# One transpose a head for both key tiles in the last eight attention blocks

## The chip, the cores and the metric

The kernel runs on one core of a Trainium2 chip. The metric is the device time of one execution in microseconds. Three runs of the kernel before gave 677.7, 679.01 and 679.52 us; the median is 679.01 us. The engines are named as in the profile: PE (TensorE, matrix products), PEld (its weight loads), DVE (VectorE), ACT (ScalarE), POOL (GpSimd), SP (the queue that issues the DMAs).

## The reference

Windowed attention with sinks, followed by two feed-forward layers over 1536 tokens of width 512:

```python
keep = (pos[None, :] < n_sink) | ((rel >= 0) & (rel < window))   # rel = query - key, n_sink 4, window 128
scores = np.where(keep, scale * (q @ k.T), -1e9)                 # 2 batches, 8 heads, 768 positions, head size 64
a = softmax(scores)                                              # with 1e-9 added to the sum
x = (a @ v) as [1536, 512]
h = x @ w_in;  x = (h * clip(h + 3, 0, 6) / 6) @ w_out           # first layer, 512 -> 2048 -> 512
h = x @ w_in2; out = (max(h, 0) + log1p(exp(-abs(h)))) @ w_out2  # second layer
```

A query at position q with window 128 sees keys q-127 to q. For a tile of 128 queries these lie in two key tiles of 128: its own (keys at or below the query's place in the tile) and the one before (keys above that place). Every place from 0 to 127 is used in exactly one of the two.

## The kernel before, in words

Attention works in 24 blocks (two heads by 256 queries), each of two units of 128 queries, so 48 units, numbered n from 0 to 47. A unit makes, for each of its two heads, a score tile of 288 columns: 128 keys of the tile before, 32 sink places, 128 keys of its own tile.

- `e_S` (line 410): four matmuls write the scores `s` to PSUM; `at_exp` (line 350) takes them off on DVE with the mask added and the row's extreme (line 355), and ACT takes the exponent with a running sum (line 359).
- `at_N` (line 364): the sum is inverted; the sink part `Ps` and the probabilities `Pt` are scaled (lines 376 to 385), from unit 16 on one head on DVE and one on ACT, in some units both on ACT.
- `e_T` (line 425): per head two PE transposes, one a key tile, into one PSUM bank `tv` (in the trace `etv`); after the second head ACT copies the whole bank to `EPT` (line 443). Units at the start of a sequence have only one key tile, and one transpose a head.
- `e_Ts` (line 447): two transposes of the sink parts and their copy. `e_V` (line 455): twelve or fewer products with v, four with the sinks' v, and the result to `X` in two parts (ACT and DVE).

`tv`, the sinks' transposes and the output of `e_V` share a pool that has a single bank (`NTV` is 1) once the first layer runs, so each has to be emptied before the next is written.

The first turns (scores of units 0 to 18) run alone at the start. The other units are woven into the first layer (`m1_h`, `m1_y`): every matmul of the layer advances a counter (`tick`), and the parts of a unit are emitted at fixed counts (`turn`, with the offsets `TH` and `TS`). The products of PE are pinned to the order in which they are written; DVE, ACT and POOL get theirs from a scheduler that orders by its own estimate of when inputs are ready. Meanwhile the weights arrive as 64-bit numbers, and each tile is turned into floats by three DVE steps (lines 28, 29, 32), two ACT steps and one POOL subtraction. The masks are made at the very start by `build_masks` (line 276) on DVE. After the attention ends, the second layer follows (`m2_h`, `m2_e`, `m2_g`, `m2_o`).

Of the kernel before, what the change touches and what calls it, by code (L numbers as in the profile page):

```python
# [8 lines left out]
F32 = mybir.dt.float32  # L9
# [3 lines left out]
AF = mybir.ActivationFunctionType  # L13
ALU = mybir.AluOpType
# [4 lines left out]
SK = 32  # L19
# [158 lines left out]
def window_attention_hardswish_softplus(  # L178
# [17 lines left out]
    nc = tc.nc  # L196
# [3 lines left out]
    P = 128  # L200
    NP = H // 2
# [6 lines left out]
    scale = 1.0 / float(D) ** 0.5  # L208
# [32 lines left out]
    negm = const.tile([P, 2 * NPU], F32, name="negm")  # L241
# [14 lines left out]
    def acopy(out_, in_, scale_=1.0, bias=0.0):  # L256
        nc.scalar.activation(out=out_, in_=in_, func=AF.Copy, scale=scale_, bias=bias)  # L257


    def pin(ins):  # L260
        return tc.keep_in_program_order(ins)
# [14 lines left out]
    def build_masks(raw, pos, mt):  # L276
        rel, col = pos[:, 0:2 * P], pos[:, 2 * P:3 * P]
        tmp = mt.tile([P, 3, 2 * P], F32, name="mtmp")
        vf = const.tile([P, 2, 2], F32, name="vf")
        nc.vector.tensor_copy(vf, raw)  # L280
        neg = const.tile([P, 2, 2], F32, name="vneg")
        nc.vector.tensor_scalar(neg, vf, 0.0, 4294967296.0, op0=ALU.is_lt, op1=ALU.mult)
        nc.vector.tensor_tensor(out=val, in0=vf[:, :, 0], in1=neg[:, :, 0], op=ALU.add)
        nc.vector.scalar_tensor_tensor(
            out=val, in0=vf[:, :, 1], scalar=4294967296.0, in1=val, op0=ALU.mult, op1=ALU.add
        )
        ns, w = val[:, 0:1], val[:, 1:2]
        k2, kn, kk = tmp[:, 0, :], tmp[:, 1, :], tmp[:, 2, :]
        big = -NEG

        def put(dst, src):
            nc.vector.tensor_scalar(dst, src, big, -big, op0=ALU.mult, op1=ALU.add)
        nc.vector.tensor_scalar(k2, rel, w, None, op0=ALU.is_lt)
        nc.vector.scalar_tensor_tensor(out=k2, in0=rel, scalar=0.0, in1=k2, op0=ALU.is_ge, op1=ALU.mult)
        nc.vector.tensor_scalar(kn[:, 0:P], col, ns, None, op0=ALU.is_ge)
        nc.vector.tensor_scalar(kn[:, P:P + SK], col[:, 0:SK], ns, None, op0=ALU.is_lt)
        m = masks[0]
        nc.vector.tensor_tensor(out=kk[:, P:], in0=k2[:, P:], in1=kn[:, 0:P], op=ALU.mult)
        put(m[:, 0:SK], kn[:, P:P + SK])
        put(m[:, SK:SK + P], kk[:, P:])  # L300
        nc.vector.memset(m[:, SK + P:], NEG)
        nc.vector.tensor_tensor(out=kk[:, 0:P], in0=k2[:, 0:P], in1=kn[:, 0:P], op=ALU.mult)
        for t, src in ((1, kk), (2, k2)):
            m = masks[t]
            put(m[:, 0:P], src[:, 0:P])
            put(m[:, P + SK:], k2[:, P:])
            put(m[:, P:P + SK], kn[:, P:P + SK])
        nc.vector.tensor_scalar(flagc[:, 0:1], ns, float(SK), None, op0=ALU.is_gt)
        nc.vector.tensor_scalar(flagc[:, 1:2], w, 1.0, None, op0=ALU.is_lt)
        nc.vector.tensor_scalar(flagc[:, 2:3], w, 128.0, None, op0=ALU.is_gt)  # L310


    AT = {}
# [21 lines left out]
    def blk(k):  # L335
        g, p = divmod(k, NP)
        b, i = divmod(g, BPB)
        return g, p, b, i

    def cols(n):  # L340
        k, i = divmod(n, 2)
        g, p, b, ib = blk(k)
        t = 2 * ib + i
        if t == 0:
            return t, 0, SK + P + SK
        if ib == 0:
            return t, SK, 2 * P + SK
        return t, i * (P + SK), 2 * P + SK

    def at_exp(n, h, s, Pt):  # L350
        t, c0, w = cols(n)
        u = 2 * n + h
        if h == 0:
            A["sum", n] = AT["ep"].tile([P, 2], F32, name="sm", tag="sm")
        nc.vector.tensor_tensor_reduce(  # L355
            out=Pt[:, h, :w], in0=s[:, :w], in1=masks[min(t, 2)][:, :w], scale=-scale, scalar=3.0e38,
            op0=ALU.add, op1=ALU.min, accum_out=negm[:, u:u + 1],
        )
        nc.scalar.activation(  # L359
            out=Pt[:, h, :w], in_=Pt[:, h, :w], func=AF.Exp, scale=-1.0, bias=negm[:, u:u + 1],  # L360
            accum_out=A["sum", n][:, h:h + 1],
        )

    def at_N(n):
        t, c0, w = cols(n)
        Pt = A["P", n]
        sm = A.pop(("sum", n))
        nc.vector.tensor_scalar(sm, sm, 1e-9, None, op0=ALU.add)
        i = nc.vector.reciprocal(sm, sm)
        if n < 4 * NP:  # L370
            stand(i)
        cs = 0 if t == 0 else P
        Ps = AT["ep"].tile([P, 2, SK], F32, name="Ps", tag="Ps")

        early = n < 4 * NP
        (nc.gpsimd if early else nc.vector).tensor_tensor(
            out=Ps, in0=Pt[:, :, cs:cs + SK], in1=sm[:, :, None].to_broadcast([P, 2, SK]), op=ALU.mult)
        A["Ps", n] = Ps
        for h in range(2):
            if early:  # L380
                nc.gpsimd.tensor_scalar(Pt[:, h, :w], Pt[:, h, :w], sm[:, h:h + 1], 1.0, op0=ALU.mult, op1=ALU.mult)
            elif h == 1 or (n < 8 * NP and n % 2 == 1):
                acopy(Pt[:, h, :w], Pt[:, h, :w], sm[:, h:h + 1])
            else:
                nc.vector.tensor_scalar(Pt[:, h, :w], Pt[:, h, :w], sm[:, h:h + 1], None, op0=ALU.mult)

# [21 lines left out]
    def e_S(n):  # L410
        k, i = divmod(n, 2)
        t, c0, w = cols(n)
        r = A["e", k]
        Pt = AT["ep"].tile([P, 2, 2 * P + SK], F32, name="Pt", tag="Pt")
        A["P", n] = Pt
        ss = [AT["eps_s"].tile([P, 512], F32, name="s", tag="s") for _ in range(2)]
        for h in range(2):
            x = r[h * D:(h + 1) * D]
            mm(out=ss[h][:, :w], lhsT=x[:, i * P:(i + 1) * P], rhs=x[:, UB + c0:UB + c0 + w], start=True, stop=True)
        for h in range(2):  # L420
            at_exp(n, h, ss[h], Pt)
        if i == 1:
            A.pop(("e", k))

    def e_T(n, h):
        k, i = divmod(n, 2)
        t, c0, w = cols(n)
        Pt = A["P", n]
        if h == 0:
            A["tv", n] = AT["eps_t"].tile([P, 2, 2, P], F32, name="etv", tag="tv")  # L430
            if i == 0:
                A["EPT", k] = (AT["ept"].tile([P, 2, 4, P], F32, name="EPT", tag="EPT"),
                               AT["ept"].tile([2 * SK, 2, P], F32, name="EPTs", tag="EPTs"))
        PT, _ = A["EPT", k]
        tv = A["tv", n]
        for j, c in ([(1, SK)] if t == 0 else [(0, 0), (1, P + SK)]):
            pin(nc.tensor.transpose(tv[:, h, j, :], Pt[:, h, c:c + P], ident))
        if h == 0:
            return
        if t == 0:  # L440
            acopy(PT[:, :, 1, :], tv[:, :, 1, :])
        else:
            acopy(PT[:, :, 2 * i:2 * i + 2, :].rearrange("p h a c -> p h (a c)"),
                  tv.rearrange("p h a c -> p h (a c)"))
        A.pop(("P", n)), A.pop(("tv", n))
# [63 lines left out]
    def stand(ins):  # L509
        after.append(ins.ins)  # L510
        del after[:-2]
# [97 lines left out]
    def turn(n):  # L609
        v = n - TL  # L610

        def scores():
            if n < 2 * NPB:
                e_S(n)
                if n % 2 == 1 and n // 2 + 3 < NPB:
                    e_load(n // 2 + 3)

        def sums():
            if v >= 2 and v % 2 == 0:
                k = v // 2 - 1  # L620
                e_V(k)
                if k + 3 < NPB:
                    e_vload(k + 3)

        def norm():
            if 0 <= v < 2 * NPB:
                at_N(v)

        todo = [(0, scores), (0, sums), (0, norm)]
        if 0 <= v < 2 * NPB:  # L630
            todo += [(TH[v % 2][h], lambda h=h: e_T(v, h)) for h in range(2)]
            if v % 2 == 1:
                todo += [(TS, lambda: e_Ts(v // 2))]
        return todo
# [34 lines left out]
    with tc.tile_pool(name="mt", bufs=1, side=left) as mt:  # L669
        pos = mt.tile([P, 3 * P], F32, name="pos")  # L670
        nc.sync.dma_start(out=pos, in_=consts[:, :3 * P])
        build_masks(raw, pos, mt)
# [240 lines left out]
```

## Time and profile before

| | |
|---|---|
| median of three runs | 679.01 us |
| profiled execution, own time | 675.99 us |
| its span from first to last instruction | 674.2 us |
| PE busy | 647.9 us, 96% |
| DVE busy | 429.0 us, 64% |
| ACT busy | 399.5 us, 59% |
| POOL busy | 109.9 us, 16% |

The profile is of one execution. Its own time is 1.8 us above its span and 3.0 us below the median of the runs. Busy shares are means over very different stages: units alone until about 60 us, first layer with conversions and attention until about 165 us, first layer with the last attention units until about 310 us, then both layers, then the second layer alone.

### The profile page before, as it was taken

The page shows a single profiled execution, that of the slowest core. Times are in us where ns is not written, and L with a number is a line of the kernel's source. Part 1 is how long each engine was busy: PE and PEld are TensorE (multiplying, and loading weights), DVE is VectorE, ACT ScalarE, POOL GpSimd, SP SyncE. Part 2 cuts the span into 40 slices and gives each one's busy share as a digit, 9 for nine tenths or more (in the row PEclk, how much of TensorE's full clock was granted, in tenths as well). Part 3 has the DMA queues.
Part 4 walks back from the last instruction along what each step waited for, and adds up shares of the span by engine and source line. Part 5 has one row for each costly group of instructions (what it writes and reads, how often), then busy time and mean ns, then how long its engine had stood idle before and what let it go on. Part 6 is the DMA issues. An engine that isn't in the chain of part 4 may idle for free.

```text
span 674.2 us, 8928 instructions
## 1 busy us (share of the span) xinstructions
PE 647.9 (96%) x3151; PEld 491.1 (73%) x3151; DVE 429.0 (64%) x899; ACT 399.5 (59%) x815; POOL 109.9 (16%) x116
## 2 busy tenths in 40 slices
PE   7897989998999999999999999999999999999995
PEld 4445657666677777777888888788788888888884
DVE  4777989887444344425677778998766545555551
ACT  3878777776554444534445557866776555565551
POOL 2663333333000000000233332222100000000000
PEclk8999999999999999999999999999999999999999
DMA  6999843111113110003866541000001000010001
GB/s 185 272 266 289 244 139 102 32 32 36 37 48 98 36 35 15 1 0 97 283 200 200 188 162 57 1 1 1 1 0 63 0 1 1 0 63 0 1 0 69
DMA packets 39541, 54.93 MB, mean 81 GB/s; under 512 B 3136, under 2 KB 29504, under 8 KB 39232
## 3 DMA queue, kind: packets, MB, share of 16 engines
q1 hardware_dynamic: 39488, 54.28, 27.0%
q8 instruction: 27, 0.44, 0.3%
q14 instruction: 26, 0.21, 0.1%
HBM read 49.02 MB, written 5.24 MB: 80 GB/s over the span
## 4 chain that ended last, share of the span: by engine, by line
PE 56%; DVE 24%; ACT 13%; issue 4%; POOL 1%; DMA 1%; SPq 0%; ACTq 0%; POOLq 0%; DVEq 0%
PE o L774 15%; PE h L738 13%; PE y L264 10%; PE hp L264 9%; DVE wraw L29 4%; DVE wraw L32 4%; DVE wraw L28 3%; DVE G L254 3%; ACT wraw L31 3%; PE etv L264 3%; PE s L264 2%; ACT w L257 2%; PE h L264 2%; ACT Pt L359 2%; ACT G L257 2%
## 5 line engine op out<-in xcount | busy, mean ns | idle before, releaser
L264 PE MATMUL y<-G,w 128*128 128x512 f32 x576 | 152.3, 400 | 0.0
L254 POOL TENSOR_TENSOR w<-wraw,w 128x512 fp32r<-128x512 f32 x64 | 87.2, 1370 | 345.6 <-ACT w L257 335.0
L774 PE MATMUL o<-w,G 128*128 128x512 f32 x576 | 138.7, 391 | 0.3 <-DVE G L254 0.3
L774 PEld LDWEIGHTS o<-w,G 128*128 128x128 f32 x576 | 108.1, 188 | 24.0 <-DVE G L254 0.7
L264 PEld LDWEIGHTS y<-G,w 128*128 128x128 f32 x576 | 104.6, 188 | 21.8 <-issue 2.3
L264 PE MATMUL hp<-X,w 128*128 128x512 f32 (+1 forms) x444 | 117.0, 399 | 2.8 <-DVE r L568 2.2
L264 PEld LDWEIGHTS hp<-X,w 128*128 128x128 f32 x444 | 78.0, 188 | 27.8 <-issue 9.6
L738 PE MATMUL h<-X,w 128*128 128x512 f32 x384 | 92.2, 389 | 0.0
L359 ACT ACTIVATE Pt<-Pt,negm 128x288 f32<-128x288 f32 (+1 forms) x96 | 49.3, 516 | 57.6 <-DVE negm L355 56.9
L738 PEld LDWEIGHTS h<-X,w 128*128 128x128 f32 x384 | 72.1, 188 | 15.0
L254 DVE TENSOR_TENSOR G<-r,G 128x512 fp32r<-128x512 f32 x48 | 43.9, 915 | 52.5 <-ACT G L257 52.4
L31 ACT ACTIVATE wraw<-wraw 128x512 f32<-128x512 f32 x64 | 43.1, 676 | 55.3 <-DVE wraw L29 55.2
L759 DVE SCALAR_TENSOR_TENSOR r<-r,ab 128x512 f32<-128x512 f32 x48 | 37.3, 776 | 38.8 <-ACT r L257 38.6
L32 DVE SCALAR_TENSOR_TENSOR wraw<-wraw 128x512 int32<-128x512 int32 x64 | 49.7, 779 | 11.9 <-ACT wraw L31 10.3
L355 DVE CUSTOM_DVE_ANT_0 Pt<-s,mask 128x288 f32<-128x288 f32 (+1 forms) x96 | 38.7, 435 | 28.8 <-PE s L264 28.4
L748 ACT ACTIVATE l<-ab 128x512 f32<-128x512 f32 x48 | 30.3, 632 | 35.8 <-DVE G L254 35.8
L257 ACT ACTIVATE w<-wraw 128x512 fp32r<-128x512 f32 x64 | 42.4, 671 | 12.8 <-DVE wraw L32 11.8
L760 DVE SCALAR_TENSOR_TENSOR l<-h,l 128x512 f32<-128x512 f32 x48 | 33.1, 689 | 24.7 <-ACT l L748 24.7
L738 PE MATMUL h<-Y,w 128*128 128x512 f32 x192 | 47.0, 395 | 0.1
L29 DVE SCALAR_TENSOR_TENSOR wraw<-wraw 128x512 int32<-128x512 int32 x64 | 46.4, 740 | 0.9
L254 DVE TENSOR_TENSOR G<-l,G 128x512 fp32r<-128x512 f32 x48 | 33.0, 688 | 21.3 <-ACT G L257 21.3
L257 ACT ACTIVATE G<-l 128x512 fp32r<-128x512 f32 x48 | 30.1, 628 | 24.9 <-PE o L774 22.8
(77 smaller groups left out, 750.0 us busy)
## 6 DMA issues: line engine op xcount, KB each, us to landing
wraw<-w_in_dram SPq DMA_DIRECT2D x32, 512.0 KB, 4.9
wraw<-w_out_dram SPq DMA_DIRECT2D x32, 512.0 KB, 4.4
eqk<-qk_dram SPq DMA_DIRECT2D x32, 176.0 KB, 3.2
ev<-vt_dram SPq DMA_DIRECT2D x16, 192.0 KB, 4.1
eqk<-qk_dram SPq DMA_DIRECT2D x16, 144.0 KB, 3.0
yd<-r SPq DMA_DIRECT2D x8, 256.0 KB, 2.9
yr<-yd SPq DMA_DIRECT2D x2, 1024.0 KB, 5.6
out_dram<-yr SPq DMA_DIRECT2D x2, 1024.0 KB, 4.2
```

The costliest lines, as they stand in the source:

```text
L29: nc.vector.scalar_tensor_tensor(out=lo, in0=hi, scalar=-2147483648, in1=lo, op0=ALU.bitwise_and, op1=ALU.bitwise_or)
L31: nc.scalar.activation(out=hi.bitcast(F32), in_=hi.bitcast(F32), func=AF.Copy, scale=WS)
L32: nc.vector.scalar_tensor_tensor(out=hi, in0=hi, scalar=3, in1=lo, op0=ALU.logical_shift_left, op1=ALU.bitwise_or)
L254: return eng.tensor_tensor(out=out_, in0=a, in1=b, op=ALU.subtract)
L257: nc.scalar.activation(out=out_, in_=in_, func=AF.Copy, scale=scale_, bias=bias)
L264: return pin(nc.tensor.matmul(**kw))
L355: nc.vector.tensor_tensor_reduce(out=Pt[:, h, :w], in0=s[:, :w], in1=masks[min(t, 2)][:, :w], scale=-scale, scalar=3.0e38, op0=ALU.add, op ...
L359: nc.scalar.activation(out=Pt[:, h, :w], in_=Pt[:, h, :w], func=AF.Exp, scale=-1.0, bias=negm[:, u:u + 1], accum_out=A["sum", n][:, h:h + 1],)
L738: nc.tensor.matmul(out=hp, lhsT=w[:, a, kk, :], rhs=Y[:, kk, e, :], start=(kk == 0 and j == 0), stop=(kk == KD - 1 and j == 2))
L759: nc.vector.scalar_tensor_tensor(out=d, in0=d, scalar=-1.0, in1=ab, op0=ALU.add, op1=ALU.subtract)
L760: nc.vector.scalar_tensor_tensor(out=l, in0=hp, scalar=0.0, in1=l, op0=ALU.max, op1=ALU.add)
L774: nc.tensor.matmul(out=M["o", b][t], lhsT=G[:, e, t * P:(t + 1) * P], rhs=w[:, a, :], start=(m == 0 and j == 0), stop=(m == KF - 1 and j = ...
```

## The change

It concerns the units from n = 32 on (`n >= 8 * NP`) that have two key tiles: sixteen units, the last eight blocks. There the two key tiles share 128 places. `at_exp` still takes 288 columns off PSUM for each head. After the second head DVE takes the minimum of the two key tiles' columns for both heads at once (masked columns hold a huge number, and the sign is turned in the exponent), written over the columns of the own tile; the exponent and the scaling then go over 160 columns instead of 288. `e_T` makes one transpose a head. Behind it DVE, instead of ACT, writes `EPT`: the transposed tile, read twice, times two triangles of ones (`sides`) that give each place to the key tile that it belongs to. The triangles are built at the start by two DVE instructions.

```diff
+        sides = AT["sides"] = AT["ep"].tile([P, 2, P], F32, name="sides", tag="sides", bufs=1)
+        nc.vector.tensor_scalar(sides[:, 0, :], rel[:, P:], 0.0, None, op0=ALU.is_gt)
+        nc.vector.tensor_scalar(sides[:, 1, :], rel[:, P:], 0.0, None, op0=ALU.is_le)
...
+        if not merged(n):
+            e_exp(n, h, Pt, slice(0, w))
+        elif h == 1:
+            nc.vector.tensor_tensor(out=Pt[:, :, P + SK:], in0=Pt[:, :, P + SK:], in1=Pt[:, :, :P], op=ALU.min)
+            for j in range(2):
+                e_exp(n, j, Pt, slice(P, w))
+    def merged(n):
+        return n >= 8 * NP and cols(n)[0] > 0
+
+    def e_exp(n, h, Pt, c):
+        u = 2 * n + h
         nc.scalar.activation(
-            out=Pt[:, h, :w], in_=Pt[:, h, :w], func=AF.Exp, scale=-1.0, bias=negm[:, u:u + 1],
+            out=Pt[:, h, c], in_=Pt[:, h, c], func=AF.Exp, scale=-1.0, bias=negm[:, u:u + 1],
...
+        c = slice(P if merged(n) else 0, w)
...
-                acopy(Pt[:, h, :w], Pt[:, h, :w], sm[:, h:h + 1])
+                acopy(Pt[:, h, c], Pt[:, h, c], sm[:, h:h + 1])
             else:
-                nc.vector.tensor_scalar(Pt[:, h, :w], Pt[:, h, :w], sm[:, h:h + 1], None, op0=ALU.mult)
+                nc.vector.tensor_scalar(Pt[:, h, c], Pt[:, h, c], sm[:, h:h + 1], None, op0=ALU.mult)
...
-        for j, c in ([(1, SK)] if t == 0 else [(0, 0), (1, P + SK)]):
+        one = merged(n) and t > 0
+        for j, c in ([(1, SK)] if t == 0 else [(0, P + SK)] if one else [(0, 0), (1, P + SK)]):
             pin(nc.tensor.transpose(tv[:, h, j, :], Pt[:, h, c:c + P], ident))
...
+        elif one:
+            nc.vector.tensor_tensor(out=PT[:, :, 2 * i:2 * i + 2, :],
+                                    in0=tv[:, :, 0:1, :].to_broadcast([P, 2, 2, P]),
+                                    in1=AT["sides"][:, None, :, :].to_broadcast([P, 2, 2, P]), op=ALU.mult)
         else:
             acopy(PT[:, :, 2 * i:2 * i + 2, :].rearrange("p h a c -> p h (a c)"),
```

How the instructions move is shown at three places. The first is PE around the second unit of one of the last eight blocks, from its scores `s` to the sinks' transposes (`etv<-ident,Ps`); `y` and `hp` are the first layer's outputs. Before:

```order
L264 MATMUL s<-eqk 128x288 x2
L264 MATMUL hp<-X,w 128x512 x3
L264 MATMUL y_2307<-G,w 128x512
L437 MATMUL etv<-ident,Pt 128x128 x2
L264 MATMUL y_2307<-G,w 128x512 x2
L264 MATMUL y_2308<-G,w 128x512
L437 MATMUL etv<-ident,Pt 128x128 x2
L264 MATMUL y_2308<-G,w 128x512 x2
L264 MATMUL y_2309<-G,w 128x512 x3
L264 MATMUL y_2310<-G,w 128x512 x2
L451 MATMUL etv<-ident,Ps 64x128 x2
```

and with the change:

```order
L264 MATMUL s<-eqk 128x288 x2
L264 MATMUL hp<-X,w 128x512 x3
L264 MATMUL y_2310<-G,w 128x512
L457 MATMUL etv<-ident,Pt 128x128
L264 MATMUL y_2310<-G,w 128x512 x2
L264 MATMUL y_2311<-G,w 128x512
L457 MATMUL etv<-ident,Pt 128x128
L264 MATMUL y_2311<-G,w 128x512 x2
L264 MATMUL y_2312<-G,w 128x512 x3
L264 MATMUL y_2313<-G,w 128x512 x2
L475 MATMUL etv<-ident,Ps 64x128 x2
```

Each pair of transposes has become one; nothing else on PE has moved, here or anywhere in the program.

The second place is the same unit on DVE, with buffer numbers, from taking off its scores to the layer's `G`. Before:

```order
L355 ISA Pt_2279,negm_70<-s_2280,mask2_74 128x288
L355 ISA negm_70 128x1
L355 ISA Pt_2279,negm_70<-s_2281,mask2_74 128x288
L355 ISA negm_70 128x1
L368 TENSOR_SCALAR sm_2284<-sm_2284 128x2
L369 RECIPROCAL sm_2284<-sm_2284 128x2
L376 TENSOR_TENSOR Ps_2428<-Pt_2279,sm_2284 128x64
L385 TENSOR_SCALAR Pt_2279<-Pt_2279,sm_2284 128x288
L568 SCALAR_TENSOR_TENSOR r_2301<-r_2301,hp_2269 128x512
L254 TENSOR_TENSOR G_2304<-r_2301,G_2304 128x512
```

and with the change:

```order
L359 ISA Pt_2281,negm_70<-s_2282,mask2_74 128x288
L359 ISA negm_70 128x1
L359 ISA Pt_2281,negm_70<-s_2283,mask2_74 128x288
L359 ISA negm_70 128x1
L366 TENSOR_TENSOR Pt_2281<-Pt_2281 128x2x128
L592 SCALAR_TENSOR_TENSOR r_2304<-r_2304,hp_2271 128x512
L463 TENSOR_TENSOR EPT_2251<-etv_2315,sides_134 128x2x256
L386 TENSOR_SCALAR sm_2286<-sm_2286 128x2
L387 RECIPROCAL sm_2286<-sm_2286 128x2
L394 TENSOR_TENSOR Ps_2429<-Pt_2281,sm_2286 128x64
L404 TENSOR_SCALAR Pt_2281<-Pt_2281,sm_2286 128x160
L254 TENSOR_TENSOR G_2307<-r_2304,G_2307 128x512
```

The minimum (L366) and the write of `EPT` (L463) are new, and the layer's `r` has moved up behind the minimum, ahead of the write of `EPT`. On ACT the same unit reads before:

```order
L359 ACTIVATE Pt_2279,sm_2284<-Pt_2279,negm_70 128x288 x2
L567 ACTIVATE r_2301<-hp_2269,chalf_71 128x512
L257 ACTIVATE Pt_2279<-Pt_2279,sm_2284 128x288
L257 ACTIVATE EPT_2247<-etv_2312 128x2x256
L257 ACTIVATE EPTs_2248<-etv_2328 64x256
```

and with the change:

```order
L591 ACTIVATE r_2304<-hp_2271,chalf_71 128x512
L377 ACTIVATE Pt_2281,sm_2286<-Pt_2281,negm_70 128x160 x2
L257 ACTIVATE Pt_2281<-Pt_2281,sm_2286 128x160
L257 ACTIVATE EPTs_2252<-etv_2329 64x256
```

The copy to `EPT` is gone from ACT, and the layer's `r` now goes ahead of the two exponents.

The third place is DVE at the start of the program, where the first weight tiles are converted (`wraw`) between the units that run alone. Before:

```order
L254 TENSOR_TENSOR X<-etv,X 128x256
L355 ISA Pt,negm<-s,mask_73 128x288
L355 ISA negm 128x1
L355 ISA Pt,negm<-s,mask_73 128x288
L355 ISA negm 128x1
L28 TENSOR_SCALAR wraw<-wraw 128x512
L29 SCALAR_TENSOR_TENSOR wraw<-wraw 128x512
L355 ISA Pt,negm<-s,mask_72 128x192
```

and with the change:

```order
L28 TENSOR_SCALAR wraw<-wraw 128x512
L254 TENSOR_TENSOR X<-etv,X 128x256
L359 ISA Pt,negm<-s,mask_73 128x288
L359 ISA negm 128x1
L359 ISA Pt,negm<-s,mask_73 128x288
L359 ISA negm 128x1
L29 SCALAR_TENSOR_TENSOR wraw<-wraw 128x512
L359 ISA Pt,negm<-s,mask_72 128x192
```

A conversion step has moved ahead of the unit's `X`. Some ten such conversion and sum steps on DVE, five on ACT and two weight subtractions on POOL are placed differently within this first stage; between it and unit 32 the orders agree on every engine.

## Rows read from the trace of the kernel before

**Rows 1.** Busy time by stage; columns: us, then PE, PEld, DVE, ACT, POOL, clock, DMA.

```profile
60.00:165.00 105.00, 97.28 (x507) 67.70 (x505) 90.39 (x209) 76.55 (x176) 30.97 (x24) 1.00 0.39 117
165.00:310.00 145.00, 143.99 (x757) 103.93 (x758) 60.99 (x185) 68.94 (x164) 2.62 (x2) 1.00 0.12 36
310.00:400.00 90.00, 90.00 (x399) 74.34 (x398) 64.42 (x95) 43.67 (x72) 22.48 (x17) 1.00 0.63 202
400.00:440.00 40.00, 39.87 (x172) 31.97 (x171) 37.24 (x55) 31.92 (x59) 10.63 (x8) 1.00 0.09 29
```

**Rows 2.** What PE waited for, 165 to 310 us, then 310 to 674 us.

```profile
PE etv L451 <- ACT EPT L257: 1.5, 1, 1.5
...
PE o L774 <- DVE G L254: 0.3, 1, 0.3
```

**Rows 3.** Timeline of PE around single transposes: start us, us, instruction, count.

```profile
173.11 0.27 PE L437 MATMUL etv<-ident,Pt 128*128 128x128 f32 x1
173.14 0.95 PE L264 MATMUL hp<-X,w 128*128 128x512 f32 x3
173.92 0.27 PE L437 MATMUL etv<-ident,Pt 128*128 128x128 f32 x1
```

**Rows 4.** Timeline of PE around pairs of transposes.

```profile
202.92 0.38 PE L437 MATMUL etv<-ident,Pt 128*128 128x128 f32 x2
203.06 0.94 PE L264 MATMUL y<-G,w 128*128 128x512 f32 x3
203.84 0.38 PE L437 MATMUL etv<-ident,Pt 128*128 128x128 f32 x2
```

**Rows 5.** Groups of instructions, 165 to 310 us: count, busy us, mean ns, idle before.

```profile
L437 PE MATMUL etv<-ident,Pt 128*128 128x128 f32 x70 | 13.5, 272 | 0.0
L257 ACT ACTIVATE EPT<-etv 128x512 f32<-128x512 f32 (+1 forms) x19 | 10.8, 571 | 1.0 <-PE etv L437 1.0
L254 DVE TENSOR_TENSOR X<-etv,X 128x256 fp32r<-128x256 f32 x10 | 4.2, 418 | 5.4 <-ACT X L257 5.4
L602 DVE COPY r<-y 128x512 f32<-128x512 f32 x2 | 1.4, 688 | 0.0
```

**Rows 6.** Groups over the whole span, shapes kept apart.

```profile
L254 DVE TENSOR_TENSOR G<-r,G 128x512 fp32r<-128x512 f32 x48 | 43.9, 915 | 52.5 <-ACT G L257 52.4
L359 ACT ACTIVATE Pt<-Pt,negm 128x192 f32<-128x192 f32 x16 | 7.1, 444 | 8.8 <-DVE negm L355 8.4 <-DVE sm L369 0.4
L254 POOL TENSOR_TENSOR w<-wraw,w 128x512 fp32r<-128x512 f32 x64 | 87.2, 1370 | 345.6 <-ACT w L257 335.0 <-DMA wraw<-w_out_dram 5.3 <-DMA wraw<-w_in_dram 5.3
```

**Rows 7.** Timeline of all engines around one second unit, 206.9 to 210.7 us.

```profile
206.89 0.96 PE L264 MATMUL hp<-X,w 128*128 128x512 f32 x3
207.37 0.45 DVE L355 CUSTOM_DVE_ANT_0 Pt<-s,mask 128x288 f32<-128x288 f32 x1
...
208.54 0.67 ACT L567 ACTIVATE r<-hp,chalf 128x512 f32<-128x512 f32 x1
...
208.84 0.38 PE L437 MATMUL etv<-ident,Pt 128*128 128x128 f32 x2
...
209.62 0.68 DVE L568 SCALAR_TENSOR_TENSOR r<-r,hp 128x512 f32<-128x512 f32 x1
209.84 0.58 ACT L257 ACTIVATE EPT<-etv 128x512 f32<-128x512 f32 x1
210.47 0.31 PEld L451 LDWEIGHTS etv<-ident,Ps 128*64 128x64 f32 x2
```

**Rows 8.** Timeline at the start, masks on DVE.

```profile
7.34 0.28 DVE L295 TENSOR_SCALAR mtmp<-pos,val 128x128 f32<-128x128 f32 x1
7.54 0.41 DVE L294 SCALAR_TENSOR_TENSOR mtmp<-pos,mtmp 128x256 f32<-128x256 f32 x1
...
9.54 0.34 DVE L355 CUSTOM_DVE_ANT_0 Pt<-s,mask 128x192 f32<-128x192 f32 x1
```

**Rows 9.** Timeline at a wait of PE, 166 us.

```profile
166.01 0.41 PE L451 MATMUL etv<-ident,Ps 128*64 128x128 f32 x2 [1.48 <-ACT EPT L257]
```

## The prediction

> **What bounds the kernel now.** I read the busy time by stage first. From 165 to 310 us, where the sixteen changed units lie, PE is busy 144.0 of 145 us, while DVE has 61.0 and ACT 68.9 [rows 1]. The view of waits agrees: PE waits once in this stage, 1.5 us for ACT's copy to EPT, and from 310 us to the end 0.3 us in one wait [rows 2]. A busy PE can hide slow matmuls, so I looked at starts in its timeline: here they follow one another without a hole. So in this stage time is PE's instruction stream, and an instruction taken out of it brings its end forward by the distance that it put between its neighbours. From 60 to 165 us it is otherwise: PE 97.3 and DVE 90.4 of 105 us [rows 1], two queues that wait for each other in turn. The change puts nothing there except through what happens at the start.
>
> **Transposes, the term that counts.** Sixteen units lose one transpose for each of two heads: 32 instructions, each out of a pair that stands between 512-column matmuls. The duration in the groups, 272 ns [rows 5], isn't what one costs, since matmuls overlap. The trace has both patterns, because units at the start of a sequence already have single transposes. From a pair over three matmuls to the next pair: 203.84 - 202.92 = 0.92 us [rows 4]. From a single over three matmuls to the next single: 173.92 - 173.11 = 0.81 us [rows 3]. Clock and matmuls are alike, so the second transpose costs 0.11 us, and 32 x 0.11 = 3.5 us go from PE. The lower bound, were each view's last digit against me, is 32 x 0.09 = 2.9; the upper, the whole duration, 32 x 0.272 = 8.7. I take 3.5, the measured distance.
>
> The Trainium skill, "TensorE: Matmul & The Clock Gate", Part 4: PE-mode transpose, says that a 128x128 transpose measured some 275 ns in a kernel's context, most of it access latency. The 272 ns here agree as a duration; by it as the price the sum would be an estimated 32 x 0.275 = 8.8 us, which the distances of rows 3 and 4 contradict.
>
> **The write of EPT moves from ACT to DVE.** ACT's copy takes 0.57 us [rows 5]. DVE's product reads PSUM and writes 512 columns; nothing in the trace reads one PSUM tile twice by a repeated pattern, so I bound it: 0.57 from below (ACT's copy), 0.92 from above (the 512-wide subtraction `G<-r`, mean 915 ns, a mean that holds stages where POOL runs too [rows 6]). I take 0.69, DVE's copy of 512 columns from PSUM [rows 5], and keep the ends. The minimum over 256 columns I put at 0.42, DVE's 256-column subtraction from PSUM in this stage [rows 5]. Together 1.11 us a unit, 17.8 us in all; the scaling over 160 instead of 288 columns gives a little back, which I leave out. DVE goes from 61 to 79 of 145 us. It has room, so the load itself costs nothing; only a place in the queue can.
>
> That place is the single PSUM bank: EPT must be written before the sinks' transposes load. In the sample second unit, PE's last transposes of the unit start at 208.84 and the sinks' load at 210.47 [rows 7]. With the change, singles bring the first to 208.73 and the second to 210.25. DVE ends its second take-off at 207.37 + 0.45 = 207.82 and the minimum at 208.24. Ahead of EPT it now has the layer's `r`, which waits for ACT. `hp` ends at 206.89 + 0.96 = 207.85; ACT, which now does `r` ahead of the exponents, takes 0.67 to 208.55 (before: 208.54 + 0.67 = 209.21, behind them). DVE's `r` of 0.68 ends at 209.25, EPT at 209.94, 0.3 us ahead of the load. At 0.92 us EPT ends at 210.17, still in time. Before, ACT ended at 209.84 + 0.58 = 210.42 [rows 7], so the new way is the earlier one. In a block's first unit EPT can start at 203.84 + 0.27 = 204.1 [rows 4], and the bank's next user, the second unit's first transpose, comes one pair (0.92) before 208.84, at 207.9: three microseconds to spare. Cost: 0, with a cover of 0.3 us a block; if it is gone, the stall is repeated in eight blocks.
>
> **Exponents.** They wait for the minimum now, so the first starts about 0.8 us later in its unit (take-off of the second head 0.4, minimum 0.4), and the pair shortens: 444 ns at 192 columns [rows 6], a bit less at 160. Behind them stand the scaling and, two turns later, the transposes, some 15 us on. Nothing on PE feels it. ACT loses sixteen copies, 9.1 us, and part of the exponents, where it had idle time anyway. No DMA and no queue of SP is touched; `sides` takes room in a pool that is freed at the attention's end.
>
> **The start.** Two 128-column DVE steps stand ahead of the masks. A step of that width takes 7.54 - 7.34 = 0.20 us to the next, 0.28 in duration, and the first take-off of scores follows the masks at 9.54 [rows 8]. So everything behind begins 2 x 0.20 = 0.4 us later; bounds 0 (a wait elsewhere in this chain of small waits swallows it) and 0.6. In the same stage the scheduler has placed some conversion steps elsewhere. The pieces that move are a 0.7 us step on DVE or a 1.37 us subtraction on POOL [rows 6], in a stage where all engines wait for each other; two such subtractions either way give -2.7 to +2.7. I take 0, since the first moved step goes into a gap and splits a pair that stood ahead of a take-off, while others move the opposite way.
>
> **Sum.** -3.5 + 0 + 0.4 + 0 = -3.1 us. The profiled execution would go from 675.99 to 672.9; the median of the runs, 679.01, lies 3.0 above it, so the forecast is 675.9. Behind 310 us everything is triggered by PE's progress, so the stream keeps the gain.
>
> **Rivals.**
> *The second layer swallows it.* From 400 to 440 us DVE is busy 37.2 of 40 [rows 1] and gives PE its one wait there [rows 2]. Were DVE's pace set by something that doesn't shift with PE, the 3.5 us would be waited off: 679.0 + 0.4, say 679.4. Against it: conversions start when PE frees weight tiles, so they shift too.
> *The start eats it.* If the moved subtractions cost their 2.7 us, 678.6. For it: 60 to 165 us has little slack on DVE. Against it: the moves are few, and of both signs.
> *DVE comes too late for the bank, slower.* A wait of the sinks' transposes for EPT is in the trace, 1.48 us at 166.01 [rows 9]. It comes back in each of eight blocks if the product takes over 0.69 + 0.3 = 1.0 us in the stream, or if `r` stays behind the exponents. At 1.5 us each that is 12 - 3.1 = 8.9 more, 687.9; the sign turns at 0.4 us a block, a product of 1.4 us. Against it: no 512-column DVE group of these reaches 1.0.
> *The full duration counts.* 32 x 0.272 - 0.4 = 8.3 less, 670.7; for it is only the duration.
>
> **Numbers.** Forecast 68%, its own range 674.2 to 677.4 (0.4 and the moves). Second layer 8%, start 12%, bank 7%, full duration 5%. About 0.3%, 2.0 us, is what a measurement of this kernel can tell from no change. Faster: 61 points of the forecast and the 5 of the full duration, 0.66. Same: 7 of the forecast, 8, and 10 of the start, 0.25. Slower: 7 and 2 of the start, 0.09. The range goes up to 679.2 to take in the start's case and most of the second layer's, and down to 673.6 for the moves' good side.
>
> **What would show it.** Right: starts from one single to the next over three matmuls at 0.81 in all sixteen units; PE busy all of a stage from 165 to about 307; no wait of the sinks' transposes for DVE; EPT on DVE near 0.69; the first take-off near 9.9 us. Wrong: waits of PE for DVE's EPT, a DVE product over 1 us, new PE holes near 430, or first layer matmuls that begin over 1 us from where they did plus 0.4.

## The result, and the profile after

The changed kernel took 672.22 us, median of six runs (670.33 to 673.69), against 678.96 for six runs of the kernel before (675.57 to 679.52): a ratio of 0.9911 (95%: 0.9887 to 0.9936). It is faster by 6.7 us by the medians and by 6.0 by the ratio, with an interval of 4.3 to 7.7; the forecast was 3.1 less, and 672.22 lies below the range's low end of 673.6. The sign was right, the size was not.

The profiled execution took 670.33 us (span 668.5), against 675.99 (674.2). Set against the same points of the program, its 5.7 us come in three pieces, at the start, in the changed stage and behind the last matmul. The first scores of unit 32, the first changed unit, begin at 167.30 instead of 168.18 us: 0.88 earlier, where the forecast had them 0.4 later. PE's timeline there, before and then after (start us, us, instruction):

```profile
168.18 0.76 PE L264 MATMUL s<-eqk 64*128 64x288 f32 x4
```

After:

```profile
167.30 0.51 PE L264 MATMUL s<-eqk 64*128 64x288 f32 x2
```

From there to the second layer's first product with its input `Y` it is 225.28 instead of 229.22 us: 3.94 less, where the forecast said 3.5. This stretch is called the stage below. That product, before and then after:

```profile
397.40 2.96 PE L738 MATMUL h<-Y,w 128*128 128x512 f32 x12
```

After:

```profile
392.58 2.73 PE L762 MATMUL h<-Y,w 128*128 128x512 f32 x11
```

From there to the last matmul these two executions are alike (269.33 against 269.46), but over all the executions below this piece runs from 268.5 to 270.8 us. The last 0.71 lies in what comes after the last matmul; that piece varies from 6.6 to 7.9 us from execution to execution, and no cause is sought for either.

The stages of [rows 1], in the trace after (busy us of PE, PEld, DVE, ACT, POOL, then clock, DMA, GB/s):

```profile
60.00:165.00 105.00, 96.45 (x502) 67.22 (x500) 89.76 (x207) 76.92 (x176) 31.28 (x24) 1.00 0.36 114
165.00:310.00 145.00, 144.87 (x746) 104.51 (x747) 79.07 (x224) 58.03 (x153) 2.27 (x2) 1.00 0.13 39
310.00:400.00 90.00, 90.00 (x399) 74.36 (x398) 64.93 (x94) 43.88 (x72) 25.52 (x19) 1.00 0.62 200
400.00:440.00 40.00, 40.00 (x173) 32.09 (x172) 38.00 (x56) 32.36 (x59) 9.35 (x8) 1.00 0.06 22
```

In the changed stage DVE stands at 79.07 us, the forecast's 79; ACT has lost 10.9; PE is as full as before. PE's waits from 165 us on are those of [rows 2], with not one new entry:

```profile
PE etv L475 <- ACT EPT L257: 1.5, 1, 1.5
PE o L798 <- DVE G L254: 0.3, 1, 0.3
```

Two single transposes in the second unit of a changed block, in place of pairs like those of [rows 4] (start us, us, instruction):

```profile
206.27 0.27 PE L457 MATMUL etv<-ident,Pt 128*128 128x128 f32 x1
206.30 0.94 PE L264 MATMUL y<-G,w 128*128 128x512 f32 x3
207.07 0.27 PE L457 MATMUL etv<-ident,Pt 128*128 128x128 f32 x1
```

From the one to the next it is 0.80 us, as [rows 3] had it (0.81). The same unit on DVE, ACT and PE's weight loads, which answers to [rows 7]:

```profile
206.22 0.43 DVE L366 TENSOR_TENSOR Pt<-Pt 128x256 f32<-128x256 f32 x1
206.24 0.69 ACT L591 ACTIVATE r<-hp,chalf 128x512 f32<-128x512 f32 x1 [2.09 <-PE hp L264]
206.96 0.69 DVE L592 SCALAR_TENSOR_TENSOR r<-r,hp 128x512 f32<-128x512 f32 x1 [0.31 <-ACT r L591]
207.56 0.68 DVE L463 TENSOR_TENSOR EPT<-etv,sides 128x512 f32<-128x512 f32 x1
208.57 0.35 PEld L475 LDWEIGHTS etv<-ident,Ps 128*64 128x64 f32 x2
```

The minimum, then `r` behind ACT, then the product: the order that the forecast set out. The product ends at 207.56 + 0.68 = 208.24, and the sinks' load comes at 208.57: 0.33 us of cover, where 0.3 was forecast. The new groups and the shortened exponents of this stage (count, busy us, mean ns, idle before):

```profile
L463 DVE TENSOR_TENSOR EPT<-etv,sides 128x512 f32<-128x512 f32 x16 | 11.0, 687 | 10.4 <-PE etv L457 10.4
L366 DVE TENSOR_TENSOR Pt<-Pt 128x256 f32<-128x256 f32 x16 | 7.4, 464 | 0.6
L377 ACT ACTIVATE Pt<-Pt,negm 128x160 f32<-128x160 f32 x32 | 13.4, 420 | 25.4 <-DVE Pt L366 25.4
```

The product's 687 ns is the 0.69 that was taken; the minimum's 464 is 44 ns over the 0.42.

### The profile page after: what moved, and what is told of

Same layout as the page of the kernel before. It is cut to its first block, busy times and chain, and to the rows that moved or that the text cites. A ratio compares the mean times of both kernels' runs of the same rounds, so it can differ in the third digit from the quotient of the medians.

```text
span 668.5 us, 8872 instructions
## 1 busy us (share of the span) xinstructions
PE 643.9 (96%) x3119; PEld 487.7 (73%) x3119; DVE 445.0 (67%) x933; ACT 386.0 (58%) x799; POOL 110.4 (17%) x116
## 4 chain that ended last, share of the span: by engine, by line
PE 60%; DVE 24%; ACT 11%; issue 3%; DMA 1%; SPq 0%; POOL 0%; ACTq 0%; POOLq 0%; DVEq 0%
PE o L798 15%; PE h L762 13%; PE y L264 12%; PE hp L264 10%; DVE wraw L29 4%; PE h L264 4%; DVE wraw L32 3%; DVE wraw L28 3%; DVE G L254 3%; PE etv L264 3%; ACT wraw L31 2%; PE s L264 2%; ACT Pt L377 2%; ACT w L257 2%; DVE Pt L359 2%
## 5 line engine op out<-in xcount | busy, mean ns | idle before, releaser
L264 PE MATMUL y<-G,w 128*128 128x512 f32 x576 | 149.6, 400 | 0.0
L31 ACT ACTIVATE wraw<-wraw 128x512 f32<-128x512 f32 x64 | 43.1, 677 | 54.7 <-DVE wraw L29 52.2
L377 ACT ACTIVATE Pt<-Pt,negm 128x288 f32<-128x288 f32 (+2 forms) x96 | 45.8, 478 | 45.9 <-DVE Pt L366 25.4
```

What stands on the lines that cost most here:

```text
L31: nc.scalar.activation(out=hi.bitcast(F32), in_=hi.bitcast(F32), func=AF.Copy, scale=WS)
L264: return pin(nc.tensor.matmul(**kw))
L377: nc.scalar.activation(out=Pt[:, h, c], in_=Pt[:, h, c], func=AF.Exp, scale=-1.0, bias=negm[:, u:u + 1], accum_out=A["sum", n][:, h:h + 1],)
```

## The experiments

Two questions were open: why the stage gave 3.94 and not 3.5, and why the start came earlier and not later. The letters in the expectations are the theories of the run concerned, and each text names its own. The first four ran together.

**The change again.** No edit.

> The change unaltered, in a second profiled execution beside the next three. In the first one the scores of unit 18 began at 54.23 us (before: 55.10), those of unit 32 at 167.30 (before: 168.18), and the span was 668.5 against 674.2. Theory A (the order of the conversion steps makes the start shorter): 54.2 and 167.3 again within 0.2. Theory B (the start differs between executions by chance): anything from 54.2 to 55.5. Time against the kernel before: a ratio near 0.991 under A; under B nearer to 0.9935 (4.4 us, the stage's part alone).

Measured: 672.46 us, ratio 0.9927 (0.9905 to 0.995), so 5.0 us (3.4 to 6.4). The stage repeated exactly, 225.29 us, but unit 18 began at 55.65, outside the ranges of both theories, and unit 32 at 168.71, 1.41 later than in the first execution of the same kernel. The busy time from 12 to 20 us, in columns as for the stages, shows what differs: first before, then the change, then this second execution of the change.

```profile
12.00:20.00 8.00, 7.15 (x41) 4.10 (x42) 3.35 (x17) 4.74 (x17) 5.20 (x14) 0.79 0.86 267
```

The change:

```profile
12.00:20.00 8.00, 7.09 (x41) 4.10 (x42) 3.76 (x19) 4.87 (x18) 5.27 (x14) 0.79 0.83 266
```

The second execution of the change:

```profile
12.00:20.00 8.00, 7.00 (x32) 4.05 (x34) 3.04 (x17) 4.57 (x18) 4.72 (x12) 0.57 0.85 260
```

The granted clock is at the lower of its two levels (1.2 GHz, 0.5 in the records) for 8 x 0.21 / 0.5 = 3.4 us in the first two and 8 x 0.43 / 0.5 = 6.9 in the third (6.8 by the trace's own record of the clock). So a start may be compared with another only where this stretch is equally long. Before and the change, with 0.79 each, may be compared, and the 0.88 stands.

**Triangles alone.** Before, with the two steps that build `sides`, which nothing uses.

```diff
+        sides = AT["sides"] = AT["ep"].tile([P, 2, P], F32, name="sides", tag="sides", bufs=1)
+        nc.vector.tensor_scalar(sides[:, 0, :], rel[:, P:], 0.0, None, op0=ALU.is_gt)
+        nc.vector.tensor_scalar(sides[:, 1, :], rel[:, P:], 0.0, None, op0=ALU.is_le)
```

> The kernel before plus the two DVE steps that build the triangles, which nothing reads; DVE, ACT and POOL get the change's order in the first stage and the old order behind it. Theory A: unit 18 begins at 54.2, the span is 0.9 shorter than before, 673.3, ratio 0.9987. Theory B: unit 18 at 55.1 to 55.5 (the two steps cost 0 to 0.4), span 674.2 to 674.6, ratio 1.000.

Measured: 676.32 us, ratio 0.9982 (0.9968 to 0.9995), so 0.3 to 2.2 us less by the medians with two instructions more. Ten of its twelve runs have a mean granted clock over 0.990, against nine of the 23 runs of before beside them; at like clock, over 0.990, the means are 676.3 and 676.5 us, so most of that difference goes with the clock. Unit 18 began at 55.46, by its figure in theory B's range, and unit 32 at 168.56; but the clock was down for 6.8 us, as in the second execution of the change (55.65 and 168.71). The stage kept 229.06. The change's start is here without the shared places; that it is shorter than before's at an equally long stretch is shown further below, at unit 16.

**Triangles on POOL.** The change, with `sides` built by POOL. The conversion steps then stand as before.

```diff
-        nc.vector.tensor_scalar(sides[:, 0, :], rel[:, P:], 0.0, None, op0=ALU.is_gt)
-        nc.vector.tensor_scalar(sides[:, 1, :], rel[:, P:], 0.0, None, op0=ALU.is_le)
+        nc.gpsimd.tensor_scalar(sides[:, 0, :], rel[:, P:], 0.0, None, op0=ALU.is_gt)
+        nc.gpsimd.tensor_scalar(sides[:, 1, :], rel[:, P:], 0.0, None, op0=ALU.is_le)
```

> The change with the triangles built on POOL, which idles at the start; the first stage then has the order of the kernel before on every engine, and the last eight blocks are as changed. Theory A: unit 18 begins at 55.1 as before, the stage from unit 32 on still gives 3.9, span 669.4 to 669.5, ratio to before near 0.9925. Theory B: no difference from the unaltered change.

Measured: 672.16 us, ratio 0.9932 (0.9915 to 0.9949); stage 225.29. Unit 32 began at 169.04, with two stretches of low clock of 6.8 us each, from 11.3 and from 52.2 us, so at unit 32 this start compares with none of the others. By the median this kernel loses nothing against the change, though 0.9 us was to be expected; intervals of 2 to 3 us can't tell. Ahead of the second stretch, at unit 16, the start does compare (below).

**Pairs back.** The change, with the second transpose of each head put back, its result unused.

```diff
-        for j, c in ([(1, SK)] if t == 0 else [(0, P + SK)] if one else [(0, 0), (1, P + SK)]):
+        for j, c in ([(1, SK)] if t == 0 else [(0, P + SK), (1, P + SK)] if one else [(0, 0), (1, P + SK)]):
```

> The change with the second transpose of each pair put back: it transposes the same shared places again, into the half of the bank that nothing reads. All else is as changed. Theory C (the transposes carry the stage's gain): 32 x 0.108 = 3.5 us of the 3.9 come back, span 672.0 against 668.5. Theory D (DVE's earlier write of EPT, or the lighter ACT, carries a good part): only a part comes back, 2 us or less.

Measured: 676.54 us, ratio 0.9989 (0.9977 to 1.0002); stage 229.38, which is 4.10 more than the change. All of the stage's gain is gone: 4.10 / 32 = 0.128 us for each transpose, and against before (229.22) the stage is 0.16 longer, so DVE's write of `EPT`, the shorter exponents and ACT's relief together give nothing. PE's timeline around two pairs of this kernel has 0.93 us (208.16 - 207.23) from one to the next:

```profile
207.23 0.38 PE L457 MATMUL etv<-ident,Pt 128*128 128x128 f32 x2
207.37 0.95 PE L264 MATMUL y<-G,w 128*128 128x512 f32 x3
208.16 0.38 PE L457 MATMUL etv<-ident,Pt 128*128 128x128 f32 x2
```

The same place in the second execution of the change has 0.80 (208.49 - 207.69):

```profile
207.69 0.27 PE L457 MATMUL etv<-ident,Pt 128*128 128x128 f32 x1
207.72 0.94 PE L264 MATMUL y<-G,w 128*128 128x512 f32 x3
208.49 0.27 PE L457 MATMUL etv<-ident,Pt 128*128 128x128 f32 x1
```

In a whole block it is 15.60 against 15.07 us: 0.53 for four transposes. 0.43 of it lies at the transposes themselves (4 x 0.108, the forecast's price). The other 0.1 is spread over the block's other matmuls, far from the transposes too: some two dozen of them start 4 to 9 ns nearer to one another. Why they do isn't shown.

**Before, once more.** No edit, one execution.

> The kernel before, unaltered, for a second profiled execution. In the runs so far the first stage differs between executions of one program by the stretch in which the granted clock is at its lower level: 3.4 us of it near 13 us in the first profiles of before and of the change, 6.8 us in the change's second, whose unit 32 began 1.41 us later (168.71 against 167.30). Theory A (order): at the same length of that stretch, before is 0.9 later than the change: 168.2 with 3.4 us, 169.6 with 6.8 us. Theory B (chance): with 6.8 us about 168.7, as the change. The stage behind, from unit 32 to the second layer's first product on Y, 229.2 under both.

Measured: 677.25 us; low clock 3.4 us from 13.8; unit 32 at 168.33, stage 229.19, as theory A had it. With the same 3.4 us at the start before now stands at 168.18 and 168.33, and kernels with the change's start at 167.30 and 167.50 (pairs back): 0.7 to 1.0 apart.

**Another start order.** Before, with the conversion step issued ahead of the transposes in the loop of the first stage, and no triangles.

```diff
+        if n in WS0:
+            w_step()
         for f in rest:
             f()
-        if n in WS0:
-            w_step()
```

> The kernel before without triangles and without merging; in the first stage a conversion step is emitted ahead of the unit's transposes and not behind its sums. From the second converted tile on DVE then has nearly the change's order; the first tile's first step stays where it was. Theory A: the start is shorter by about half of the change's 0.9 (the first tile's step gave 0.4 of it): unit 32 at 167.7 with 3.4 us of lower clock, 169.1 with 6.8; ratio to before 0.9993. Theory B, or a theory in which the triangles' place in memory does it: as before, 168.2 and ratio 1.000.

Measured: 675.82 us, ratio 0.9971 (0.9956 to 0.9986); unit 32 at 167.07 with 3.4 us of low clock, stage 229.14. The order of these steps alone, with nothing added or taken away, moves unit 32 by 1.1 us, twice what was expected. The first tile's step stayed where it was, and the take-off behind it comes no earlier than before (22.16 there):

```profile
22.26 0.35 DVE L355 CUSTOM_DVE_ANT_0 Pt<-s,mask 128x192 f32<-128x192 f32 x1
```

So what this order gives comes from the later tiles alone.

**The product twice.** The change, with DVE's write of `EPT` done twice.

```diff
+            for _ in range(2):
                 nc.vector.tensor_tensor(out=PT[:, :, 2 * i:2 * i + 2, :],
...
```

> The change with DVE's product that writes EPT done twice, one behind the other; orders are otherwise the change's. It tests the cover that the prediction put at 0.3 us a block (0.33 in the change's trace: product ends at 208.24, the load of the sinks' transposes starts at 208.57). Theory F (the cover is as read): the second product of 0.62 to 0.69 makes PE wait about 0.3 in each of eight blocks, 2.4 to 2.9 us more in the stage from unit 32: 227.7 to 228.2 instead of 225.3. Theory G (PE's queue has more slack than that): below 1 us.

Measured: 675.38 us, ratio 0.9964 (0.9947 to 0.9982); stage 228.03, 2.75 more than the change, 0.34 in each of eight blocks. This tests the cover. In the second of them the second product ends at 209.92 + 0.69 = 210.61, and the load follows 0.12 us behind (columns as above; the bracket is the idle time before):

```profile
209.20 0.68 DVE L464 TENSOR_TENSOR EPT<-etv,sides 128x512 f32<-128x512 f32 x1
209.92 0.69 DVE L464 TENSOR_TENSOR EPT<-etv,sides 128x512 f32<-128x512 f32 x1
210.73 0.14 PEld L476 LDWEIGHTS etv<-ident,Ps 128*64 128x64 f32 x2 [0.56 <-issue]
```

The view doesn't name the product as what the load waited for. It puts PE's new waits in the stage, seven in all, down to the next step in DVE's queue (us in total, times, longest):

```profile
PE etv L476 <- DVE sm L387: 1.2, 7, 0.3
```

An added 0.69 less the cover of 0.33 is 0.36, and 0.34 was measured. The rival by which DVE comes too late for the bank had its place right; it decides from 0.33 us on, not here.

**From unit 16 on.** The change, with twelve more units merged.

```diff
-        return n >= 8 * NP and cols(n)[0] > 0
+        return n >= 4 * NP and cols(n)[0] > 0
```

> The change applied to all units with two key tiles from unit 16 on, twelve more units, 24 more transposes gone. Between 60 and 165 us PE is not saturated and DVE has 90 of 105 us. Theory H (this stage also runs at PE's pace): 24 x 0.128 = 3.1 us less than the change, span 665.4 to 666.6. Theory I (it runs at DVE's pace): twelve times 1.1 us more DVE work less what ACT's relief gives, 5 to 13 us more than the change, 674 to 681.

Measured: 678.33 us, ratio 1.0003 (0.9989 to 1.0018), about 6 us over the change. From 60 to 165 us, where DVE had 89.76 us of 105, it now has 96.29 (columns as for the stages):

```profile
60.00:165.00 105.00, 95.24 (x476) 65.40 (x477) 96.29 (x218) 65.58 (x159) 30.37 (x23) 0.95 0.39 116
```

PE's longest wait there is for DVE's scaling (us in total, times, longest):

```profile
PE etv L457 <- DVE Pt L404: 5.0, 1, 5.0
```

Within that wait the granted clock falls, and it stays at its lower level for 10.2 us from 59.7:

```profile
58.00:70.00 12.00, 9.09 (x44) 7.11 (x46) 6.05 (x19) 4.66 (x17) 2.35 (x2) 0.57 0.91 241
```

All twelve runs have a mean clock of 0.985 to 0.988, below most runs of the other kernels. Theory I's range is met: twenty-four transposes less on PE don't pay where DVE's queue sets the pace. How much of the 6 us is DVE's added work and how much the low clock isn't told apart.

**The change with the other start order.** The edit of the other start order, made in the change.

> The change with the conversion step emitted ahead of the unit's transposes in the first stage, as in the sixth run; on DVE one 0.7 us step then stands behind a take-off and not ahead of it, on ACT some steps move. Theory A (the start's length is set by these orders): the start is no longer than the change's at the same stretch of lower clock, unit 32 at 166.9 to 167.5 with 3.4 us of it or 168.3 to 168.9 with 6.8; the stage behind 225.3 as in the change; time within 0.6 us of the change, ratio to before 0.991 to 0.9935.

Measured: 673.19 us, ratio 0.9941 (0.9923 to 0.996); stage 225.29. Unit 32 began at 169.04 with a second stretch of low clock, 6.8 us from 57.4. At unit 16, ahead of that stretch, it stands at 47.54, where the change's two executions with 3.4 us of low clock have 47.33 and 47.50. No better than the change: what an order gives depends on the other order it is joined with, and it doesn't add up.

**Before, two more executions.** No edit.

> The kernel before, a third profiled execution. Theory A: unit 32 at 168.2 to 168.4 if the early stretch of lower clock is 3.4 us long, at 169.5 to 169.8 if it is 6.8; with a second such stretch near 52 us, as in the third run, up to 1 us later still. Theory B: no relation to these stretches.

> The kernel before, a fourth profiled execution, with the expectations of the one ahead of it.

Measured: 675.6 and 679.2 us of one kernel on one chip. Unit 32 begins at 168.40 in the first and 170.89 in the second, inside and 0.1 above theory A's ranges, and 2.5 of the 3.6 us between them; the stage differs by 0.17 (229.24 and 229.41), and 0.9 lies between the stage and the last matmul (268.83 and 269.75). The second has the long stretch of low clock at the start and another one near 60 us:

```profile
12.00:20.00 8.00, 7.13 (x34) 3.97 (x34) 2.93 (x16) 4.44 (x17) 4.77 (x13) 0.59 0.84 262
50.00:58.00 8.00, 5.66 (x40) 2.74 (x38) 7.57 (x22) 6.84 (x18) 4.35 (x6) 1.00 1.09 249
58.00:70.00 12.00, 11.12 (x59) 8.49 (x60) 5.87 (x24) 8.12 (x22) 2.55 (x2) 0.72 1.09 285
```

Ahead of the fall PE is busy 5.66 of 8 us. That alone doesn't tell why: the second execution of the change has 5.31 there and keeps its clock from 58 to 70 us:

```profile
50.00:58.00 8.00, 5.31 (x38) 2.64 (x38) 7.57 (x22) 6.85 (x19) 3.90 (x5) 1.00 1.10 266
58.00:70.00 12.00, 10.74 (x69) 8.01 (x70) 7.48 (x27) 9.12 (x24) 2.56 (x2) 1.00 1.08 294
```

In the first that other stretch was 3.4 us long and left unit 32 within 0.1 to 0.2 of the executions without it.

The second of these gives what was lacking so far, an execution of before with the long early stretch. Unit 16 begins ahead of every second stretch (the earliest falls at 52.23), so there the starts of all kernels with the same steps on PE compare. Its first scores in us, by the order of the steps on DVE and by the length of the early low clock:

| order of the start | 3.4 us | 6.8 us |
|---|---|---|
| as before | 48.20, 48.25, 48.27 | 49.00 (triangles on POOL), 49.20 |
| as in the change | 47.33, 47.50 | 48.41, 48.49, 48.55 (triangles alone), 48.74 |
| other order, in before and in the change | 47.09, 47.54 | |

Three of them as the timeline has them, before with the long stretch, then triangles on POOL, then triangles alone:

```profile
49.20 0.51 PE L264 MATMUL s<-eqk 64*128 64x288 f32 x2
```

Triangles on POOL:

```profile
49.00 0.51 PE L264 MATMUL s<-eqk 64*128 64x288 f32 x2
```

Triangles alone:

```profile
48.55 0.51 PE L264 MATMUL s<-eqk 64*128 64x288 f32 x2
```

At like clock no start with before's order is as early as one with the change's: they lie 0.70 to 0.94 apart with the short stretch and 0.26 to 0.79 with the long one. The triangles on POOL, which keep the shared places and give back the old order, go with before.

**More filler at the start.** The change, with four instead of two filler matmuls of one kind at the start, to raise PE's activity there.

```diff
-    NWU, NWV, NWT = 8, 12, 2
+    NWU, NWV, NWT = 8, 12, 4
```

> The change with four filler products a turn and not two on PE in the first stage, to keep PE busier there. Theory J (the stretches of lower clock come from PE's idle time and cost up to 1.4 us): they get shorter or vanish, the start shrinks by up to 1.4 less what the filler takes (34 more products of 0.11), time 0 to 1.4 below the change. Theory K (the filler stands in the way of the chain, or the changed orders undo the gain of the start): 0 to 4 us above the change.

Measured: 672.48 us, ratio 0.9935 (0.9914 to 0.9956); unit 32 at 168.34 with 3.4 us of low clock, so the filler costs 1.0 and buys nothing that the median shows. All eleven of its runs have a mean clock over 0.990, against seven of twelve of the change; so with more filler the long low stretches seem rarer, as theory J had it, though the profiled execution keeps its 3.4 us, and the filler's own cost takes the gain back. None of the kernels tried goes below the change by more than the intervals.

## Why the prediction was wrong

**What bounds the kernel: right.** PE's stream set the changed stage, and what went out of it came back in full at the second layer's first product with `Y`: no wait was added, and from 310 us on [rows 2] repeats itself. How much of it is left at the end the traces can't tell to better than the 2 us by which that last piece varies; the times say that most is.

**"32 x 0.11 = 3.5 us go from PE": the term was mis-sized.** It is 3.94 by the change, and 4.10 by the pairs put back. The distance of [rows 3, 4] measures a transpose between two like places, and there it is right (0.108). The stream's other matmuls moved closer as well, 0.1 us a block, which a distance between neighbours can't hold. The lesson is one of size, not of method: the full duration, the rival at 8.7 us, is refuted. The Trainium skill ("TensorE: Matmul & The Clock Gate", Part 4: PE-mode transpose) states some 275 ns in one kernel's context. That holds as a duration (272 here, before and after), and it is more than twice the price that the pairs put back show, 128 ns.

**The write of EPT, the exponents: right.** DVE's load (79.07), the product (687 ns), the queue's order, ACT's earlier `r` and the cover of 0.33 came as worked out, and the doubled product, 0.34 us a block against the 0.36 that the cover gives, agrees with it. (The prediction's additions run 0.05 us high on the way: by its own rows the product ends at 209.89 and not 209.94, a cover of 0.36.) The bounds of 0.57 and 0.92 were needlessly wide: the repeated pattern costs nothing, 687 ns against the 688 of a plain copy [rows 5]. The Trainium skill ("VectorE: DVE Perf Modes", "The TRN2 errata") states (N + 151)/0.96 ns for an fp32 `tensor_tensor` add, as exact for 512 and 2048 columns. An estimate by it is 691 ns for 512 columns; the 687 of the product agrees. For the minimum over 256, which reads SBUF alone and in pieces of 128, the same estimate is 424 where 464 were measured, so there the trace differs; the subtraction for `X`, also 256 wide, takes 418 [rows 5].

**"So everything behind begins 2 x 0.20 = 0.4 us later", and "I take 0" for the moved steps: this is the step that failed.** The first half: the two steps took 0.14 us each to the next and not 0.20, the first take-off came at 9.67, 0.13 later and not 0.4, and the little chain of waits behind it swallowed that (the last reciprocal ahead of the lines below begins at 19.01 instead of 19.00). The second half has the wrong sign. DVE near 20 us, before:

```profile
19.00 0.17 DVE L369 RECIPROCAL sm<-sm 128x2 f32<-128x2 f32 x1
19.54 0.42 DVE L254 TENSOR_TENSOR X<-etv,X 128x256 fp32r<-128x256 f32 x1 [0.38 <-ACT X L257]
20.34 0.46 DVE L355 CUSTOM_DVE_ANT_0 Pt<-s,mask 128x288 f32<-128x288 f32 x1 [0.37 <-POOL Pt L381]
...
21.10 0.42 DVE L28 TENSOR_SCALAR wraw<-wraw 128x512 int32<-128x512 int32 x1
21.55 0.69 DVE L29 SCALAR_TENSOR_TENSOR wraw<-wraw 128x512 int32<-128x512 int32 x1
22.16 0.35 DVE L355 CUSTOM_DVE_ANT_0 Pt<-s,mask 128x192 f32<-128x192 f32 x1
```

And after:

```profile
19.10 0.47 DVE L28 TENSOR_SCALAR wraw<-wraw 128x512 int32<-128x512 int32 x1
19.56 0.42 DVE L254 TENSOR_TENSOR X<-etv,X 128x256 fp32r<-128x256 f32 x1
...
20.69 0.69 DVE L29 SCALAR_TENSOR_TENSOR wraw<-wraw 128x512 int32<-128x512 int32 x1
21.43 0.36 DVE L359 CUSTOM_DVE_ANT_0 Pt<-s,mask 128x192 f32<-128x192 f32 x1
```

DVE was idle for 0.38 us ahead of `X` and 0.37 ahead of the take-off, waiting for ACT and POOL. The conversion's first half (0.47) now stands in the first of these gaps, and `X` follows at 19.56 instead of 19.54. The wait for POOL is gone as well; why, the trace doesn't show. So the take-off behind the conversion's second half comes at 21.43 instead of 22.16, 0.73 earlier. A second such split follows, other steps move both ways, and by unit 32 it is 0.88. The prediction saw this very move ("goes into a gap and splits a pair that stood ahead of a take-off") and set it at nothing against "others move the opposite way", without reading the gap's length. That the order does it, and neither the merged units nor chance, is shown at unit 16: the triangles alone have the change's start without the units, and the triangles on POOL have the units without the change's start. That an order alone can move the start by about as much is shown by the other start order. Which of the moved steps makes the 0.88 isn't shown: these two splits are read from the trace, and the other start order gives 1.1 without the first of them. The prediction's own mark for failure, first matmuls over 1 us from "plus 0.4", was met: 0.88 + 0.4 = 1.28.

**The rest of the miss.** The forecast lies 3.7 us above the median. The start makes 0.88 + 0.4 = 1.28 of it, the transposes 0.44. Another 1.4 is the base: the sum was set against a median of three runs, 679.01, and 71 later runs of before have a mean of 677.6. That leaves 0.6, which the scatter hides: the piece from the stage to the last matmul has a mean of 269.0 us over five executions with the change's stage and 269.9 over six with before's, each over a range of more than 1 us. The runs list their mean granted clock. Of the 71, 29 had over 0.990, mean 676.7 us; 42 had 0.990 or less, mean 678.3. Of twelve runs of the change, seven had over 0.990, mean 671.8; five less, mean 672.8. At like clock the change gains 4.9 and 5.5 us; the first is near 3.94 + 0.88 = 4.8, and both measured intervals (4.3 to 7.7 and 3.4 to 6.4) hold 4.8. Before has the lower clock in 42 of 71 runs and the change in five of twelve; with 1.6 us between the groups of before that would be 0.3 us more. Five of twelve is few, but the kernels that share the change's start and leave the units ahead of 32 alone (the change, triangles alone, pairs back, product twice) have 35 of 47 runs over 0.990, against 29 of 71 of before and two of six with the triangles on POOL. So the higher clock goes with the change's start; how the one brings the other about isn't shown, and what brings the second stretch on was not found.

**The rivals.** The second layer kept nothing back: PE 40.00 of 40 us from 400 us on. The start did not eat the gain, it added to it. DVE was in time for the bank in every block. The full duration's 670.7 comes within some 1.5 us of the median, by luck: its 8.7 us for the transposes are refuted by the 3.94 and 4.10 of the stage.

## What to carry to other kernels

Price an instruction that leaves a full PE by the distance that it puts between its neighbours in the trace, not by its duration, and expect some more from the rest of the stream (here up to a fifth). Where the change lets a scheduler place other steps anew, read for each moved step the idle time at its old and its new place: a step that moves into a wait can be a gain, and here the moved steps together gave a fifth of the change's own. Before two executions are compared, compare the granted clock in their first tens of microseconds.

## What was not expected of the hardware

One kernel's executions differ in how long the granted clock is low near 12 us, 3.4 or 6.8 us, and the longer one costs 1.41 us at unit 32 (167.30 against 168.71, the change twice); of the 3.6 us between two executions of before, 679.2 and 675.6, the start with its stretches makes 2.5. Two instructions at the start whose result nothing reads brought unit 16 forward by 0.45 to 0.65 us at like clock (48.55 against 49.00 and 49.20), by the order that they left behind. And a DVE product that reads one PSUM tile twice by a repeated pattern costs what a plain one of its width does: 687 ns for 512 columns.
